# Softmax division moved behind the value products in the first attention block of a fused attention and MLP kernel

## The chip, the cores and the metric

The kernel runs on one core of a Trainium2 chip. The metric is the device time of one execution in microseconds (us); lower is better. The median of three runs of the kernel before is 956.29 us (956.23 to 956.37). Engines are named as the profile names them: PE is TensorE (matmuls), PEld its weight loads, DVE is VectorE, ACT is ScalarE, POOL is GpSimd, SP the queue that issues the DMAs.

## The reference

Three stages run one after the other: windowed causal attention with a distance penalty per head, a two-matrix MLP with a clipped gate, and a gated MLP behind an RMS norm. The change touches the attention alone.

```python
B, H, S, D = 4, 8, 576, 64            # attention; window 128
scores = q @ k.T / sqrt(D)
scores = where(0 <= i - j < 128, scores - slope[h] * |i - j|, -1e9)
attn = exp(scores - max(scores))
attn = attn / (sum(attn) + 1e-9)
x = (attn @ v) reshaped to (B*S, H*D) = (2304, 512)
h = x @ w_in                          # 512 -> 2048
x = (h * clip(h + 3, 0, 6) / 6) @ w_out
xn = x / rms(x) * rms_g
out = (silu(xn @ w_gate) * (xn @ w_val)) @ w_out2   # 512 -> 1536 -> 512
```

## The kernel before

The 2304 tokens are 18 tiles of 128 rows (`P`), in six blocks of three tiles (`BLOCKS`). For every block, attention makes the transposed input `xs` of the first MLP (four chunks `c` of 128 features, a high and a low part each), and the first MLP follows it as 16 products `ps_h` (`product1`, L484) and 16 times three products `ps_o` (`product2`, L497). Attention for the first block has nothing in front of it to run beside: it has its own loop of 15 slots (`AHEAD`, L577 to L599). Attention for the later blocks runs inside the MLP loop of the block before.

Attention goes by pairs of heads (`Pair`, index `j` from 0 to 3 in a block) and steps (`Step`, one query tile `u` of a pair against 256 keys; the first tile of a batch sees 128 keys). So the first block is 12 steps; step s belongs to pair s // 3. In slots 12 to 14 the loop also starts the three steps of the next block's first pair. A step passes through four stages, in slots that a table gives (`plan`, L437), one slot apart:

- S, slot s: `scores` (L357), two fp32 matmuls, one for each head of the pair, into `ps_s`; `bias` (L371) on DVE adds the penalty out of PSUM and takes the row extreme `m`; `exp` (L386) on ACT makes weights `t` and their row sum `den`; two instructions on POOL (L388, L389) make `r = 1 / (den + 1e-9)`.
- D, slot s + 1: `divide` (L394), two DVE instructions that multiply `t` by `r`.
- T, slot s + 2: `transpose` (L400), two or four PE transpositions of 128x128 blocks of `t` into the one bank `ps_t`; `weights` (L405) copies them to `pt` on ACT.
- V, slot s + 3: `values` (L418), two or four fp32 matmuls with 64 columns of `vraw` stationary and `pt` moving, which add into the pair's accumulator `ps_av`, already turned to features by queries. All pairs of the block use one bank, tag "A".
- With a pair's last V: `finish` (L327 on ACT, L328 on DVE) splits the accumulator into the high and low part of `xs`, and the next `vraw` but one is loaded (L297).

Each engine runs its own queue in program order, so the order of the lines in the loop is the order of the work. Within a slot of the loop before it is: scores, transpositions, values, copies of weights, bias, scaling of a coming pair's q (L304, with the loads of k and q of a later pair on SP), divisions, finish, exponentials. Behind them in slots 4, 5, 7, 8, 9 and 11 stand the pieces of `W1.step`, the conversion of the first MLP's weights: L131, L136 and L145 on ACT, L140, L143 and L147 on DVE.

An fp32 matmul stands in the trace as two records, a PE transposition as one. The two heads' matmuls of a step use different halves of the array, in `scores` the rows and in `values` the columns.

Of the kernel before, what the change touches and what calls it, by code (L numbers as in the profile page):

```python
# [10 lines left out]
F32 = mybir.dt.float32  # L11
# [4 lines left out]
AF = mybir.ActivationFunctionType  # L16
# [4 lines left out]
P = 128  # L21
# [39 lines left out]
EARLY = {0: 1, 1: 3, 2: 6, 3: 8, M2 - 1: 11}  # L61
PAIRS2 = NTILE // 6

KINDS = "QSDTLV"

OPEN = {"reuse_waits": "tile"}

# [6 lines left out]
def fused_kernel(ctx: ExitStack, tc: tile.TileContext, qd, kd, v, w1, w2, rms_g, out):  # L74
# [201 lines left out]
    class Pair:  # L276
# [17 lines left out]
        def load_v(self):  # L294
            j, k0, nk = self.j, self.lo * P, self.nch * P
            self.vr = ap.tile([P, 4, P], F32, tag="v", name="vraw", bufs=2)
            sp.dma_start(  # L297
                out=self.vr[:, : self.nch],
                in_=v[k0 : k0 + nk, j * P : (j + 1) * P].rearrange("(c p) d -> p c d", p=P),
            )  # L300

        def scale(self):
            q = self.qr[:, : self.n * P]
# [26 lines left out]
    class Step:  # L330
# [12 lines left out]
        def scores(self):  # L343
            pr, c0, k0 = self.pair, self.c0, (self.i - 1 - self.pair.lo) * P
            for x, y in PARTS_OF if pr.parts else ():
                for a, s in enumerate(self.s):
                    rows = slice(a * D, (a + 1) * D)
                    pe.matmul(  # L348
                        s[:, c0:],
                        lhsT=pr.qs[rows, x, self.u * P : (self.u + 1) * P],  # L350
                        rhs=pr.ks[rows, y, k0 + c0 : k0 + 2 * P],
                        start=(x == 0 and y == 0),
                        stop=(x == 1),
                    )
            for a, s in enumerate(self.s if not pr.parts else ()):
                rows = slice(a * D, (a + 1) * D)
                pe.matmul(  # L357
                    s[:, c0:],
                    lhsT=pr.qr[rows, self.u * P : (self.u + 1) * P],
                    rhs=pr.kr[rows, k0 + c0 : k0 + 2 * P],  # L360
                    start=True,
                    stop=True,
                )
# [16 lines left out]
                pool.memset(self.t[:, :, :HALF], 0.0)  # L380

        def exp(self):
            self.den = small.tile([P, 2], F32, tag="den", name="den")
            for a in range(2):
                p = self.t[:, a, self.p0 :]
                act.activation(p, p, AF.Exp, bias=self.m[:, a : a + 1], scale=-1.0, accum_out=self.den[:, a : a + 1])  # L386
            self.r = small.tile([P, 2], F32, tag="r", name="r")
            pool.tensor_scalar(self.r, self.den, 1e-9, None, ALU.add)  # L388
            pool.tensor_tensor(self.r, self.r, minus, ALU.pow)  # L389
# [12 lines left out]
        def weights(self):  # L402
# [3 lines left out]
            for c, sign in ((0, -1), (1, 1)) if self.joint else ():  # L406
# [2 lines left out]
                    base=c - 1, pattern=[[0, 2], [sign, P]], channel_multiplier=-sign,  # L409
                )  # L410

        def values(self):
            pr = self.pair
            if pr.acc is None:
                pr.acc = ps_a.tile([P, 3, P], F32, tag="A", name="ps_av")
            for c in range(self.from_, 2):
                for a in range(2):
                    pe.matmul(  # L418
                        pr.acc[a * D : (a + 1) * D, self.u],
                        lhsT=pr.vr[:, self.i - 1 + c - pr.lo, a * D : (a + 1) * D],  # L420
                        rhs=self.pt[:, a, c],
                        start=(c == self.from_),
                        stop=(c == 1),
                        skip_group_check=True,
                    )
# [8 lines left out]
    for k, pr in enumerate(pairs):  # L434
        b, j = divmod(k, H // 2)
        if b < 2:
            t0, plan = 3 * j if b == 0 else AHEAD - 3 + 3 * j, {"S": (0, 1, 2), "D": (1, 2, 3), "T": (2, 3, 4), "V": (3, 4, 5)}  # L437
        else:
            t0, plan = AHEAD + M1 * (b - 1) - 2 + 4 * j, {"S": (0, 0, 0), "D": (1, 1, 2), "T": (None, 2, 3), "L": (1, None, None), "V": (5, 5, 5)}
        slots["Q"].setdefault(t0 - (2 if b < 2 else 1), []).append(pr)  # L440
        for u in range(pr.n):
            step = Step(pr, u)
            for kind, at in plan.items():
                if at[u] is not None:
                    slots[kind].setdefault(t0 + at[u], []).append(step)

    def at(t):
        return [slots[kind].get(t, []) for kind in KINDS]

# [125 lines left out]
    busy(WARM)  # L575
    pairs[0].scale()
    for t in range(AHEAD):  # L577
        q, s_, d_, t_, _, v_ = at(t)
        scores(s_, t % 2)
        for x in t_:  # L580
            x.transpose()
        for x in v_:
            x.values()
        for x in t_:
            x.weights()
        for x in s_:
            x.bias()
        prepare(q, s_)
        for x in d_:
            x.divide()  # L590
        for x in v_:
            if x.last:
                finish(x.pair)
        for x in s_:
            x.exp()
        if t == 2:
            W1.load(3)
        W1.step(0, *{4: (0,), 5: (1, 2), 7: (3,), 9: (4, 5)}.get(t, ()))
        W1.step(1, *{8: (0,), 11: (1, 2)}.get(t, ()))  # L599
# [83 lines left out]
    for p, (b, m0, m1) in enumerate(PARTS):  # L683
# [13 lines left out]
        xs = xs_of[b]  # L697
        for m in range(m0, m1):
            t, slot = slot, slot + 1
            q, s_, d_, t_, l_, v_ = at(t)  # L700
            go = p < 3 or last or (t - AHEAD) % 4 in (0, 3)
            if p == 3 and m == 2:
                first.close()
# [301 lines left out]
```

## Time and profile before

| | |
|---|---|
| median of 3 runs | 956.29 us |
| span of the profiled execution | 954.2 us |
| PE busy | 937.7 us, 98% of the span |
| PE weight loads | 832.9 us, 87% |
| DVE, ACT, POOL busy | 640.5, 454.2, 186.3 us |
| the first 40th of the span: PE busy | 7 tenths; from the third 40th on 9 tenths |
| chain that ended last | PE 87%, DVE 6%, ACT 4% |

The span goes from the first instruction to the last; what the runs show above it lies around it. A busy share is the part of the span in which at least one instruction of the engine was under way. The page's view of 40 slices has each slice's busy share in tenths, about 24 us a slice. The chain of waits is followed back from the last instruction to whatever released it. A timeline row has the start, the duration of the group, engine, line, operation, and in square brackets how long the engine was idle before it and what released it.

### The profile page before, as it was taken

The numbers are of one execution on the slowest core, as the hardware profiler recorded it, in microseconds if no ns is written. First come the engines' busy times: TensorE is split into PE (matmuls) and PEld (weight loads), VectorE is DVE, ScalarE is ACT, GpSimd is POOL, SyncE is SP. The second block draws the span as 40 slices with busy tenths as digits, with TensorE's granted clock in tenths as the row PEclk, the third lists the DMA queues.
The fourth block names the chain that finished last, engine by engine and source line by source line (L and its number), as shares of the span: only waits on it lengthen the run. The fifth ranks groups of instructions, "written<-read, shape, count | busy, mean of one in ns | idle before, by whom it ended". The sixth has DMA issues, their size and how long they took to land.

```text
span 954.2 us, 14654 instructions
## 1 busy us (share of the span) xinstructions
PE 937.7 (98%) x5336; PEld 832.9 (87%) x5336; DVE 640.5 (67%) x1336; ACT 454.2 (48%) x969; POOL 186.3 (20%) x327
## 2 busy tenths in 40 slices
PE   7899999999999999999999999999999999999998
PEld 4587888888888888888899999999999999999996
DVE  5788667555878777877467657777545577545555
ACT  6899566455666655655455453433131323231120
POOL 4333012332223332422124223310000000000000
PEclk8999999999999999999999999999999999999999
DMA  6555401113666555554355757866757555755521
GB/s 231 183 194 194 187 20 51 32 53 117 198 211 203 172 164 174 164 169 130 122 182 210 287 206 293 320 229 234 249 212 281 214 202 199 265 206 211 214 86 67
DMA packets 67432, 175.02 MB, mean 183 GB/s; under 512 B 5024, under 2 KB 41888, under 8 KB 62624
## 3 DMA queue, kind: packets, MB, share of 16 engines
q1 hardware_dynamic: 67360, 174.09, 52.2%
q8 instruction: 42, 0.69, 0.3%
q14 instruction: 30, 0.25, 0.1%
HBM read 130.03 MB, written 44.04 MB: 182 GB/s over the span
## 4 chain that ended last, share of the span: by engine, by line
PE 87%; DVE 6%; ACT 4%; issue 2%; POOL 1%; ACTq 0%; POOLq 0%; DVEq 0%
PE ps_o L497 19%; PE ps_h L484 18%; PE ps_y L892 15%; PE ps_o L845 10%; PE ps_S L845 8%; PE ps_A L845 6%; PE ps_h L845 4%; PE ps_av L418 2%; PE ps_t L400 2%; PE ps_s L357 1%; DVE wx L143 1%; PE ps_s L348 1%; ACT t L386 1%; ACT wx L136 1%; DVE t L371 1%
## 5 line engine op out<-in xcount | busy, mean ns | idle before, releaser
L497 PE MATMUL ps_o<-w,g 128*128 128x512 f32 x864 | 224.0, 402 | 2.1 <-DVE w L147 1.9
L484 PE MATMUL ps_h<-xs,w 128*128 128x384 f32 x1152 | 220.2, 339 | 0.0
L484 PEld LDWEIGHTS ps_h<-xs,w 128*128 128x128 f32 x1152 | 202.4, 188 | 5.8 <-issue 0.2
L497 PEld LDWEIGHTS ps_o<-w,g 128*128 128x128 f32 x864 | 156.2, 188 | 41.1 <-issue 6.3
L892 PE MATMUL ps_y<-wo,g 128*128 128x512 f32 x648 | 150.2, 390 | 0.5 <-DVE g L881 0.5
L892 PEld LDWEIGHTS ps_y<-wo,g 128*128 128x128 f32 x648 | 121.3, 188 | 25.1 <-DVE g L881 0.9
L723 DVE SCALAR_TENSOR_TENSOR t<-t,ps_h 128x384 f32<-128x384 f32 x96 | 53.2, 554 | 98.7 <-ACT t L722 98.6
L722 ACT ACTIVATE t<-ps_h,three 128x384 f32<-128x384 f32 x96 | 55.5, 578 | 84.1 <-PE ps_h L484 80.2
L899 DVE TENSOR_TENSOR y<-y,ps_y 128x512 f32<-128x512 f32 x90 | 61.7, 686 | 35.3 <-PE ps_y L892 35.0
L386 ACT ACTIVATE t<-t,m 128x128 f32<-128x128 f32 (+1 forms) x144 | 61.4, 428 | 29.4 <-DVE t L378 14.2
L728 ACT CAST g<-t 128x384 fp32r<-128x384 f32 x96 | 49.5, 516 | 47.5 <-DVE t L723 46.2
L734 DVE TENSOR_TENSOR g<-t,g 128x384 fp32r<-128x384 f32 x96 | 54.4, 567 | 23.3 <-ACT g L728 23.0
L868 ACT ACTIVATE r<-r 128x384 f32<-128x384 f32 x36 | 19.0, 527 | 105.6 <-DVE r L867 105.6
L845 PE MATMUL ps_o<-S,tw 128*128 128x384 f32 x336 | 66.2, 339 | 0.3 <-DVE t L865 0.3
L388 POOL TENSOR_SCALAR r<-den 128x2 f32<-128x2 f32 x72 | 27.4, 380 | 187.6 <-ACT t L386 186.0
L845 PEld LDWEIGHTS ps_o<-S,tw 128*128 128x128 f32 x336 | 59.3, 188 | 1.4 <-DVE u L856 0.8
L389 POOL TENSOR_TENSOR r<-r,minus 128x2 f32<-128x2 f32 x72 | 56.0, 778 | 6.0
L407 POOL TENSOR_SCALAR_AFFINE_SELECT pt<-pt 128x256 f32<-128x256 f32 x82 | 34.5, 421 | 107.5 <-ACT pt L405 104.5
L853 ACT COPY s<-ps_S 128x384 f32<-128x384 f32 x18 | 8.7, 481 | 86.9 <-PE ps_S L845 86.9
L371 DVE CUSTOM_DVE_ANT_0 t<-ps_s,rel 128x256 f32<-128x256 f32 (+2 forms) x128 | 45.2, 395 | 3.6 <-PE ps_s L357 3.6
L143 DVE SCALAR_TENSOR_TENSOR wx<-wx,wy 128x512 uint32<-128x512 uint32 (+1 forms) x52 | 44.2, 850 | 0.0
L136 ACT ACTIVATE wx<-wraw 128x512 f32<-128x512 f32 (+1 forms) x52 | 42.8, 824 | 0.0
(138 smaller groups left out, 1471.9 us busy)
## 6 DMA issues: line engine op xcount, KB each, us to landing
tw<-t SPq DMA_DIRECT2D x52, 896.0 KB, 6.3
wraw<-w SPq DMA_DIRECT2D x36, 512.0 KB, 4.1
wo<-w SPq DMA_DIRECT2D x18, 1024.0 KB, 4.9
wraw<-w SPq DMA_DIRECT2D x16, 1024.0 KB, 9.1
t<-th SPq DMA_DIRECT2D x12, 896.0 KB, 4.3
t<-tl SPq DMA_DIRECT2D x12, 896.0 KB, 4.3
b<-wx SPq DMA_DIRECT2D x24, 256.0 KB, 2.6
w<-w SPq DMA_DIRECT2D x12, 512.0 KB, 3.0
```

What stands on the lines that cost most here:

```text
L143: vec.scalar_tensor_tensor(out=xi, in0=xi, scalar=3, in1=y, op0=ALU.logical_shift_left, op1=ALU.bitwise_or)
L371: vec.tensor_tensor_reduce(out=self.t[:, a, c0:], in0=s[:, c0:], in1=(rel_split if self.i in SPLITS else rel)[:, c0:], scale=2.0 ** (-8.0 ...
L386: act.activation(p, p, AF.Exp, bias=self.m[:, a : a + 1], scale=-1.0, accum_out=self.den[:, a : a + 1])
L389: pool.tensor_tensor(self.r, self.r, minus, ALU.pow)
L484: pe.matmul(ps[:, : n * P], lhsT=w[:, a, c * P : (c + 1) * P], rhs=xs[c][:, b, : n * P], start=(k == 0), stop=(k == 3 * KC - 1),)
L497: pe.matmul(o, lhsT=g[:, a, i * P : (i + 1) * P], rhs=w[:, b], start=(m == first and a == 0 and b == 0), stop=(m == last and a == 1),)
L722: act.activation(r[:, :nq], ps[:, :nq], AF.Relu, bias=three)
L723: vec.scalar_tensor_tensor(out=r[:, :nq], in0=r[:, :nq], scalar=6.0, in1=ps[:, :nq], op0=ALU.min, op1=ALU.mult)
L734: vec.tensor_sub(g[:, 1, :nq], r[:, :nq], f32(g[:, 0, :nq]))
L845: pe.matmul(ps, lhsT=w[a][:, k, c * P : (c + 1) * P], rhs=x[:, b, c], start=(start and j == 0), stop=(j == 5), skip_group_check=True,)
L892: pe.matmul(ps, lhsT=gs[i + k][:, a, t // 3, t % 3 * P : (t % 3 + 1) * P], rhs=wo[i + k][:, b], start=(k == 0 and a == 0 and b == 0), stop ...
L899: vec.tensor_add(acc[t], acc[t], ps)
```

## The change

In the first block alone, the weights are no longer divided before they are turned. `exp` only exponentiates, without the row sums and without the two POOL instructions. The stages are S, T, V and X in slots s, s + 1, s + 2 and s + 3. T turns the raw weights. V is `rows`: the turned weights are now stationary (128 columns), and the moving operand is 65 columns of v, 64 and a column of ones, so that each product has 128 queries as rows and the row sum in its 65th column. Three DVE instructions then add 1e-9 to the sums, take the reciprocal and scale the rows. X is `columns`: one PE transposition of the scaled 128x128 rows into the pair's accumulator, which is bank "h" for pairs 0 and 2 and bank "A" for 1 and 3. The load of v for this block writes two halves around the column of ones, in two DMAs, behind one POOL memset. The order of the lines in the loop changes with it.

```diff
         def load_v(self):
...
+            x = v[k0 : k0 + nk, j * P : (j + 1) * P].rearrange("(c p) d -> p c d", p=P)
+            if self.b:
+                sp.dma_start(out=self.vr[:, : self.nch], in_=x)
+                return
+            self.va = self.vr.rearrange("p c d -> p (c d)")[:, : self.nch * 2 * (D + 1)]
+            self.va = self.va.rearrange("p (c a d) -> p c a d", a=2, d=D + 1)
+            pool.memset(self.va[:, :, :, D:], 1.0)
+            for a in range(2):
+                sp.dma_start(out=self.va[:, :, a, :D], in_=x[:, :, a * D : (a + 1) * D])
...
         def exp(self):
+            if self.pair.b == 0:
+                for a in range(2):
+                    p = self.t[:, a, self.p0 :]
+                    act.activation(p, p, AF.Exp, bias=self.m[:, a : a + 1], scale=-1.0)
+                return
...
+        def rows(self):
+            pr = self.pair
+            ps = ps_out.tile([P, 2, D + 1], F32, tag="o2", name="ps_rows")
+            for a in range(2):
+                for c in range(self.from_, 2):
+                    pe.matmul(
+                        ps[:, a],
+                        lhsT=self.pt[:, a, c],
+                        rhs=pr.va[:, self.i - 1 + c - pr.lo, a],
+                        start=(c == self.from_),
+                        stop=(c == 1),
+                    )
+            r = small.tile([P, 2], F32, tag="r", name="r")
+            vec.tensor_scalar(r, ps[:, :, D], 1e-9, None, ALU.add)
+            vec.reciprocal(r, r)
+            self.x = gpool.tile([P, 2, D], F32, tag="g", name="rows")
+            vec.tensor_tensor(self.x, ps[:, :, :D], r.unsqueeze(2).to_broadcast([P, 2, D]), ALU.mult)
+
+        def columns(self):
+            pr = self.pair
+            if pr.acc is None:
+                p, tag = ((ps_h, "h"), (ps_a, "A"))[pr.j % 2]
+                pr.acc = p.tile([P, 4, P], F32, tag=tag, name="ps_av")[:, :3]
+            pe.transpose(pr.acc[:, self.u], self.x.rearrange("p a d -> p (a d)"), ident)
...
+            if b == 0:
+                plan = {"S": (0, 1, 2), "T": (1, 2, 3), "V": (2, 3, 4), "X": (3, 4, 5)}
...
     for t in range(AHEAD):
         scores(s_, t % 2)
+        for x in x_:
+            x.columns()
         for x in t_:
             x.transpose()
-        for x in v_:
-            x.values()
-        for x in t_:
-            x.weights()
         for x in s_:
             x.bias()
+        for x in v_:
+            x.rows()
         prepare(q, s_)
         for x in d_:
             x.divide()
-        for x in v_:
+        for x in s_:
+            x.exp()
+        for x in t_:
+            x.weights()
+        for x in x_:
             if x.last:
                 finish(x.pair)
-        for x in s_:
-            x.exp()
```

What this does to the queue of PE in slots 7 and 8, the middle of the loop, stands in the next two pieces: first before, then changed (`ps_s` scores, `ps_t` transpositions, `ps_av` values before and columns after, `ps_rows` rows; a number at a name tells buffers apart).

```order
L357 MATMUL ps_s_369<-kraw,qraw 128x256
L357 MATMUL ps_s_370<-kraw,qraw 128x256
L400 MATMUL ps_t<-ident,t 128x128 x4
L418 MATMUL ps_av<-pt,vraw 64x128 x4
L357 MATMUL ps_s_398<-kraw,qraw 128x256
L357 MATMUL ps_s_399<-kraw,qraw 128x256
L400 MATMUL ps_t<-ident,t 128x128 x2
L418 MATMUL ps_av<-pt,vraw 64x128 x4
```

The same two slots of PE's queue in the changed kernel:

```order
L362 MATMUL ps_s_380<-kraw,qraw 128x256
L362 MATMUL ps_s_381<-kraw,qraw 128x256
L446 MATMUL ps_av<-ident,rows 128x128
L410 MATMUL ps_t<-ident,t 128x128 x2
L428 MATMUL ps_rows<-vraw,pt 128x65 x4
L362 MATMUL ps_s_408<-kraw,qraw 128x256
L362 MATMUL ps_s_409<-kraw,qraw 128x256
L446 MATMUL ps_av<-ident,rows 128x128
L410 MATMUL ps_t<-ident,t 128x128 x4
L428 MATMUL ps_rows<-vraw,pt 128x65 x2
```

A transposition of the rows (L446) now stands between the scores and the transpositions of the weights. It reads what DVE made of the rows products that stand one group of scores ahead of it.

On DVE the same stretch, slot 7 and the start of slot 8, reads before (`t` and `m` are the two results of the bias, `wx` and `wy` belong to the conversion of MLP weights):

```order
L371 ISA t,m<-ps_s_369,rel 128x256
L371 ISA m 128x1
L371 ISA t,m<-ps_s_370,rel 128x256
L371 ISA m 128x1
L304 TENSOR_SCALAR qraw<-qraw,qscale 128x384
L394 TENSOR_SCALAR t<-t,r 128x128 x2
L143 SCALAR_TENSOR_TENSOR wx<-wx,wy 128x1024
L371 ISA t,m<-ps_s_398,rel 128x256
```

and in the changed kernel:

```order
L376 ISA t,m<-ps_s_380,rel 128x256
L376 ISA m 128x1
L376 ISA t,m<-ps_s_381,rel 128x256
L376 ISA m 128x1
L436 TENSOR_SCALAR r<-ps_rows 128x2
L437 RECIPROCAL r<-r 128x2
L439 TENSOR_TENSOR rows<-ps_rows,r 128x128
L309 TENSOR_SCALAR qraw<-qraw,qscale 128x384
L143 SCALAR_TENSOR_TENSOR wx<-wx,wy 128x1024
L376 ISA t,m<-ps_s_408,rel 128x256
```

The two divisions (L394) are gone; three instructions on the rows product stand behind the bias, and the conversion (L143) keeps its place ahead of the next slot's bias.

## Rows read from the trace of the kernel before

**Rows 1.** The page: the span.
```profile
span 954.2 us, 14654 instructions
```
**Rows 2.** Busy time by stretch: stretch and length, engines, granted clock, DMA share, GB/s.
```profile
5.09:38.90 33.81, 26.76 (x186) 16.20 (x185) 23.63 (x98) 25.89 (x77) 14.15 (x28) 0.85 0.53 177
38.90:105.00 66.10, 64.26 (x390) 51.72 (x389) 55.78 (x115) 59.34 (x108) 20.81 (x25) 1.00 0.64 234
105.00:900.00 795.00, 793.97 (x4511) 718.20 (x4510) 530.26 (x1069) 359.39 (x771) 148.86 (x262) 1.00 0.53 186
```
**Rows 3.** The chain that ended last, in order of time, around 30 us.
```profile
29.95 1.10 ACT t L386 x4
...
31.13 0.23 POOL r L388
...
31.43 0.72 POOL r L389
```
**Rows 4.** Waits from 5 to 39 us: us in total, times, longest.
```profile
PE ps_t L400 <- DVE t L394: 5.7, 5, 2.4
...
PE ps_t L400 <- ACT pt L405: 0.9, 1, 0.9
...
PE ps_av L418 <- DVE xs L328: 0.2, 1, 0.2
```
**Rows 5.** Busy time by stretch again, where the granted clock changes.
```profile
8.83:15.65 6.82, 6.82 (x34) 4.20 (x34) 3.95 (x20) 4.33 (x16) 2.56 (x5) 0.50 0.94 327
15.65:32.72 17.07, 11.92 (x103) 7.07 (x100) 12.89 (x50) 14.49 (x39) 7.33 (x14) 1.00 0.39 123
32.72:36.12 3.40, 3.40 (x15) 2.09 (x16) 3.05 (x12) 3.20 (x10) 1.28 (x3) 0.50 0.26 77
```
**Rows 6.** Timeline of PE from 8 to 39 us.
```profile
8.74 0.67 PE L400 MATMUL ps_t<-ident,t 128*128 128x128 f32 x2 [1.60 <-DVE t L394]
...
24.89 0.63 PE L400 MATMUL ps_t<-ident,t 128*128 128x128 f32 x4 [1.13 <-DVE t L394]
...
26.66 0.63 PE L400 MATMUL ps_t<-ident,t 128*128 128x128 f32 x4
27.21 0.66 PE L418 MATMUL ps_av<-pt,vraw 128*64 128x128 f32 x8
27.80 0.70 PE L357 MATMUL ps_s<-kraw,qraw 64*128 64x256 f32 x4
30.87 0.30 PE L400 MATMUL ps_t<-ident,t 128*128 128x128 f32 x1 [2.37 <-DVE t L394]
...
38.90 2.35 PE L484 MATMUL ps_h<-xs,w 128*128 128x384 f32 x12
```
**Rows 7.** Timeline of PE's weight loads around 20 us.
```profile
20.07 0.42 PEld L400 LDWEIGHTS ps_t<-ident,t 128*128 128x128 f32 x4 [1.28 <-ACT pt L405]
20.66 0.42 PEld L418 LDWEIGHTS ps_av<-pt,vraw 128*64 128x64 f32 x8 [0.17 <-issue]
```
**Rows 8.** Groups by line and shape on DVE, 5 to 39 us: busy us, mean ns.
```profile
L371 DVE CUSTOM_DVE_ANT_0 t<-ps_s,rel 128x256 f32<-128x256 f32 x18 | 6.9, 421 | 2.0 <-PE ps_s L357 2.0
...
L371 DVE DVE_READ_ACCUMULATOR2_ANT m<- 128x1 f32 x30 | 2.5, 84 | 0.0
...
L371 DVE CUSTOM_DVE_ANT_0 t<-ps_s,rel 128x128 f32<-128x128 f32 x8 | 2.0, 285 | 1.6 <-PE ps_s L357 1.6
...
L147 DVE TENSOR_TENSOR w<-wx,w 128x1024 fp32r<-128x1024 f32 x1 | 1.2, 1226 | 1.5 <-ACT w L145 1.5
L143 DVE SCALAR_TENSOR_TENSOR wx<-wx,wy 128x1024 uint32<-128x1024 uint32 x1 | 1.2, 1219 | 0.0
```
**Rows 9.** Timeline of DVE at 143 us: an instruction that reads its neighbour's result.
```profile
143.10 0.42 DVE L371 CUSTOM_DVE_ANT_0 t<-ps_s,rel 128x256 f32<-128x256 f32 x1
...
143.57 0.42 DVE L378 TENSOR_TENSOR t<-t 128x256 f32<-128x256 f32 x1
```
**Rows 10.** DMA issues from 0 to 60 us: count, KB each, median us to landing.
```profile
vraw<-v SPq DMA_DIRECT2D x4, 192.0 KB, 3.5
```

More of the change, by code (lines that the diff above doesn't have):

```diff
@@ L62 @@
 PAIRS2 = NTILE // 6
-KINDS = "QSDTLV"
+KINDS = "QSDTLVX"
 OPEN = {"reuse_waits": "tile"}
@@ L296, in load_v @@
             self.vr = ap.tile([P, 4, P], F32, tag="v", name="vraw", bufs=2)
[L297 to L300, printed above, removed]
+            x = v[k0 : k0 + nk, j * P : (j + 1) * P].rearrange("(c p) d -> p c d", p=P)
[7 more added lines that the diff above has]
+                sp.dma_start(out=self.va[:, :, a, :D], in_=x[:, :, a * D : (a + 1) * D])
         def scale(self):
@@ L577, in fused_kernel @@
     for t in range(AHEAD):
-        q, s_, d_, t_, _, v_ = at(t)
+        q, s_, d_, t_, _, v_, x_ = at(t)
         scores(s_, t % 2)
+        for x in x_:
+            x.columns()
         for x in t_:
             x.transpose()
-        for x in v_:
-            x.values()
-        for x in t_:
-            x.weights()
         for x in s_:
             x.bias()
+        for x in v_:
+            x.rows()
         prepare(q, s_)
@@ L699, in fused_kernel @@
             t, slot = slot, slot + 1
-            q, s_, d_, t_, l_, v_ = at(t)
+            q, s_, d_, t_, l_, v_, _ = at(t)
             go = p < 3 or last or (t - AHEAD) % 4 in (0, 3)
```

## Prediction, made before the changed kernel ran

> **What bounds the kernel now.** I read the busy times by stretch first. From 105 us to 900 us PE is busy for 793.97 of 795 us [rows 2], so time lost or won ahead of that stretch is not made up later. The first block's attention is the stretch from the first scores at 5.09 us to the first MLP product at 38.90 us [rows 2, 6]: 33.81 us, in which PE shows 26.76 us of work at a mean granted clock of 0.85. It is the only place that the change touches. From 38.90 to 105 us PE is busy for 64.26 of 66.10 us, and the work there hangs on the slots behind the loop, so it shifts as a whole when the loop ends earlier or later.
>
> Next the chain of waits inside the loop. It alternates: exponential on ACT, then the two POOL instructions (0.23 and 0.72 us), then a division on DVE, then PE [rows 3]. The waits say the same: PE's transpositions waited 5.7 us for divisions and 0.9 us for copies, its value products 0.2 us for the split of the accumulator [rows 4], 6.8 us in all. The rest of the loss is the clock: for 6.82 and 3.40 us the granted clock was 0.50, that is 1.2 instead of 2.4 GHz, with PE busy throughout [rows 5]. Each time the fall came after PE had sat idle for long, 1.60 and 2.37 us; an idle of 1.13 us was not followed by one [rows 6].
>
> **The change part by part.** All prices are for the full clock; a step has eight records of value products if it sees two key chunks, four if it sees one (8 and 4 of the 12 steps).
>
> *Removed wait.* The division leaves the way from exponential to transposition: at most the 6.8 us [rows 4]. The second accumulator bank is in this number with its 0.2 us and can be worth no more.
>
> *Rows in place of values.* Eight value records with 64 stationary columns load in 0.42 us; four transpositions, with 128 stationary columns, need the same 0.42 us [rows 7]. So a record with 128 stationary columns takes 0.105 us where one with 64 takes 0.053. The new products have 128 stationary columns and stream 65. If the load sets the pace, eight records take 0.84 us instead of 0.42: 8 x 0.42 + 4 x 0.21 = +4.2 us. Lower bound: the transpositions' pace comes from streaming 128 columns, the loads are hidden, and 65 columns cost no more than now: 0. Upper bound: load and stream one after the other, 0.16 us a record: +8.5 us. I take 4.2, because the row with the same stationary shape is the transposition's. The Trainium skill, page "TensorE: Matmul & The Clock Gate", section "LDWEIGHTS (loading the stationary operand)", speaks against the change here: the time of a load goes with the columns of the stationary operand, about columns / 1.2 in ns, so 107 ns for 128 columns and 53 for 64. By that rule the term is 4.3 us and the time 960.3; by the streaming reading it is 0 and the time 956.0.
>
> *Turning the rows.* One transposition for each step, 0.105 us, and the 0.17 us that a group with its own wait spends on issue [rows 7]: 12 x 0.28 = +3.3 us. Without the issue time it would be 1.3.
>
> *The new wait.* The turn (L446) stands at the head of the slot, in front of the transpositions and the rows, and needs DVE's three instructions on the rows product issued just before. A group of PE delivers 0.24 us after its last load (0.66 against 0.42) [rows 6, 7]. On DVE, reading PSUM takes 421 ns at 256 columns and 285 at 128 [rows 8]; carried down to 2 columns that is an estimated 0.15 us each for the addition and the reciprocal, and 0.285 for the scaling. A reader of its neighbour's result starts 0.05 us after that ends [rows 9]. So 0.24 + 0.15 + 0.05 + 0.15 + 0.05 + 0.285, and about 0.07 for each of two hand-overs: 1.07 us. Between lies only the next group of scores, 0.43 us of issue (0.70 less the drain [rows 6]), 0.21 if narrow, with 0.17 us before and after it. PE idles 0.30 us in nine slots and 0.52 in three: +4.3 us. Bounds: 1.6 us less if the two small ones cost 84 ns, as the smallest DVE row does [rows 8]; 3.6 more if the reciprocal takes three times 0.15. The transpositions and rows queue behind this turn, and the next scores behind those.
>
> *Conversion on DVE.* L143 and L147 (1.22 and 1.23 us [rows 8]) stay between one slot's scaling and the next slot's bias. Before, they ran while PE waited anyway. Now each holds up the bias and with it the next rows' scaling, for which PE waits: about 0.95 us each after what the scores hide, +1.9. Bounds 0 and 2.4.
>
> *Left-over waits of the transpositions.* The first follows the second scores at once and waits for its exponential, the second for the copy of the first (one bank `ps_t`), the last for a division of the next block: +1.5, between 1 and 2.
>
> *End of the loop.* The last split now stands on ACT behind two exponentials and a copy, and the first MLP product needs it for its last quarter: +0.6, between 0 and 1.
>
> *The clock.* The two long idles disappear, since the first transposition no longer stands behind two divisions; no idle in the sums above passes 1.2 us. I take PE to keep 2.4 GHz, which halves 10.2 us: -5.1. This is an upper bound of the gain, as part of the slow work lay under other waits; the lower bound is 0.
>
> *Counted as nothing.* The row sums on ACT, 24 POOL instructions and 24 divisions go: the cover is that ACT and POOL are then off the way, and DVE has the new three in their place. The four POOL memsets run on an emptied POOL, and the four extra DMA issues on SP stand behind loads of k and q. A load of v lands 3.5 us after issue [rows 10] and is needed three slots later, over 6 us; if that cover went, each late load would hold PE by the difference.
>
> **Sum.** -6.8 + 4.2 + 3.3 + 4.3 + 1.9 + 1.5 + 0.6 - 5.1 = +3.9 us on the profiled span of 954.2 [rows 1], so 958.1. The median of the runs lies 2.1 us above that span, with no part of it touched: 960.2 us.
>
> **The rivals.**
>
> *Weight loads hidden.* PE loads the next weights beside the running product, and the 65 columns cost what the values did. For it: later in the trace loads are busy for 718 of 795 us beside a PE that is busy throughout [rows 2]. Against: the transpositions' pace. The sum falls by 4.2 to 956.0, no change. It decides at a spacing of 0.053 against 0.105 us. Chance 0.15.
>
> *The division is back in time* (the other sign). If the way from the last rows record to the scaled rows takes 0.77 us or less, not 1.07, the scores and their issue cover it; PE then never stands in front of the turn and the 4.3 goes, and with that slack the conversion's 1.9 as well: 954.0, faster by 0.24%. For it: DVE rows of 84 ns exist. Against: with two of these the way is still 0.94 us. Chance 0.09.
>
> *The clock falls again.* PE works with short pauses in every slot and may be granted 1.2 GHz as before. One stretch like the shorter one costs 1.7 us (961.9), all 10.2 us cost 5.1 (965.3). [...] Against: from 15.65 to 32.72 us, with a transposition group in every slot, the granted clock was 1.00 [rows 5]. Chance 0.18.
>
> *The change does not shorten the way:* v in two halves lands late. Four loads, each 0.5 us late, would add 2 us: 962.2. Chance 0.03.
>
> **How the numbers follow.** 0.2% is 1.9 us, about what a measurement of this kernel can tell from no change. The forecast, 960.2, has 0.55, and its own bounds reach from 957 to 964; a twentieth of that chance lies below 958.2. Faster: 0.09. Same: the hidden loads and that twentieth, 0.18. Slower: the rest, 0.73. The range takes in the hidden loads below and one slow stretch with dear loads above: 955.8 to 964.5. It leaves out the faster rival and the clock slow throughout.
>
> **What would show it.** Right: PE waits of `ps_av` L446 on `rows` L439 of some 0.3 us in nearly every slot, summing to 4 to 7 us; loads of L428 spaced by 0.105 us, eight in about 0.85; no POOL in the chain; a granted clock of 1.00 in the loop; the first `ps_h` product near 42.2 us. Wrong: L428 spaced by 0.053 us, or L446 without idle time before it; or a product that starts before 38 us. If the clock falls, the stretches show it.

## The result and the profile after

| | before | after |
|---|---|---|
| median of 11 runs each, us | 956.35 (955.19 to 957.65) | 960.95 |
| ratio, 95% interval | 1 | 1.0057 (1.0039 to 1.0075) |
| span of the profiled execution, us | 954.2 [rows 1] | 958.2, of a run of 959.92 |

The changed kernel is slower by 0.57%, about 5 us. Of its eleven runs one took 1314 us and is left out of the ratio, as are single runs of 3224 us in run 4 and 983 us in run 5 below; seven lie between 959.1 and 961.7 us and three between 965.4 and 966.8 us, a spread that the kernel before doesn't show.

First the page of the changed kernel: its span, and the chain that ended last by engine.

```profile
span 958.2 us, 14624 instructions
...
PE 87%; DVE 7%; ACT 4%; issue 1%; POOL 0%; ACTq 0%; POOLq 0%; DVEq 0%
```

POOL, which [rows 3] show in the chain of the loop, has 0% of it, after 1% before. Next its busy time by stretch, cut at the first scores, the first MLP product and the two changes of the granted clock (columns as in [rows 2]).

```profile
5.13:40.82 35.69, 29.09 (x198) 21.59 (x197) 23.97 (x111) 23.34 (x53) 2.25 (x7) 0.95 0.50 165
40.82:105.00 64.18, 62.50 (x368) 50.65 (x367) 53.63 (x113) 56.17 (x104) 20.34 (x23) 0.97 0.63 233
105.00:900.00 795.00, 793.67 (x4509) 716.59 (x4508) 530.49 (x1068) 360.11 (x772) 146.80 (x262) 1.00 0.53 185
...
5.13:37.50 32.37, 25.80 (x184) 19.14 (x183) 21.94 (x100) 22.62 (x51) 0.99 (x4) 1.00 0.55 181
37.50:44.30 6.80, 6.78 (x27) 5.93 (x26) 3.11 (x13) 2.35 (x9) 2.18 (x6) 0.50 0.50 154
```

From 105 to 900 us nothing changed. The loop is 35.69 us long instead of 33.81 [rows 2], and where the kernel before had two stretches at half the clock inside it [rows 5], this one has a single stretch of 6.80 us, which begins in the loop and ends in the first MLP product. The timeline of PE (start, length, instruction, count, idle time before it) shows a plain slot, the long idles with the transpositions of slots 9 (25.35 us) and 11 (31.65 us) behind them, and that product:

```profile
10.33 0.33 PE L446 MATMUL ps_av<-ident,rows 128*128 128x128 f32 x1 [0.36 <-DVE rows L439]
10.49 0.60 PE L410 MATMUL ps_t<-ident,t 128*128 128x128 f32 x4
10.93 1.00 PE L428 MATMUL ps_rows<-vraw,pt 128*128 128x65 f32 x8
11.86 0.70 PE L362 MATMUL ps_s<-kraw,qraw 64*128 64x256 f32 x4
12.71 0.33 PE L446 MATMUL ps_av<-ident,rows 128*128 128x128 f32 x1
...
24.83 0.33 PE L446 MATMUL ps_av<-ident,rows 128*128 128x128 f32 x1 [1.16 <-DVE rows L439]
25.35 0.66 PE L410 MATMUL ps_t<-ident,t 128*128 128x128 f32 x4 [0.20 <-ACT pt L415]
...
31.34 0.33 PE L446 MATMUL ps_av<-ident,rows 128*128 128x128 f32 x1 [1.58 <-DVE rows L439]
31.65 0.66 PE L410 MATMUL ps_t<-ident,t 128*128 128x128 f32 x4
...
36.37 0.33 PE L446 MATMUL ps_av<-ident,rows 128*128 128x128 f32 x1 [0.65 <-DVE rows L439]
37.08 1.61 PE L428 MATMUL ps_rows<-vraw,pt 128*128 128x65 f32 x8 [0.38 <-ACT pt L415]
...
40.82 3.94 PE L522 MATMUL ps_h<-xs,w 128*128 128x384 f32 x12
44.60 0.60 PE L410 MATMUL ps_t<-ident,t 128*128 128x128 f32 x4
```

Eight rows products take 0.93 us from start to start (10.93 to 11.86), the eight value products took 0.59 [rows 6]. The first MLP product starts 1.92 us later than before [rows 6] but takes 3.94 us instead of 2.35. The transposition behind it is 3.51 us later than in the kernel before, whose row is this:

```profile
41.09 0.60 PE L400 MATMUL ps_t<-ident,t 128*128 128x128 f32 x4
```

The waits from 5 to 46 us (us in total, times, longest), and behind the 1.58 us of idle the chain around 28 us:

```profile
PE ps_av L446 <- DVE rows L439: 4.6, 6, 1.6
...
PE ps_t L410 <- ACT pt L415: 0.6, 2, 0.4
...
PE ps_rows L428 <- ACT pt L415: 0.4, 1, 0.4
...
PE ps_t L410 <- ACT t L391: 0.2, 1, 0.2
```

```profile
27.79 0.96 ACT w L145
28.77 1.23 DVE w L147
30.00 0.33 DVE t L376
```

DVE stood first for ACT's half of the weight conversion (L145) and then took 1.23 us for its own (L147); the bias and the scaling of the rows came behind both.

### The profile page after: what moved, and what is told of

Its sections match the earlier page's. It is cut to its first block, busy times and chain, and to the rows that moved or that the text cites. A ratio compares the mean times of both kernels' runs of the same rounds, so it can differ in the third digit from the quotient of the medians.

```text
span 958.2 us, 14624 instructions
## 1 busy us (share of the span) xinstructions
PE 942.1 (98%) x5348; PEld 839.7 (88%) x5348; DVE 641.7 (67%) x1348; ACT 451.0 (47%) x945; POOL 172.1 (18%) x307
## 4 chain that ended last, share of the span: by engine, by line
PE 87%; DVE 7%; ACT 4%; issue 1%; POOL 0%; ACTq 0%; POOLq 0%; DVEq 0%
PE ps_o L535 18%; PE ps_h L522 18%; PE ps_y L932 15%; PE ps_o L885 10%; PE ps_S L885 8%; PE ps_A L885 6%; PE ps_h L885 4%; PE ps_av L454 2%; PE ps_t L410 2%; PE ps_s L362 1%; DVE wx L143 1%; ACT wx L136 1%; PE ps_s L353 1%; DVE t L763 1%; PE ps_x L588 1%
## 5 line engine op out<-in xcount | busy, mean ns | idle before, releaser
L396 ACT ACTIVATE t<-t,m 128x128 f32<-128x128 f32 (+2 forms) x120 | 50.0, 418 | 27.6 <-DVE t L383 14.5
L398 POOL TENSOR_SCALAR r<-den 128x2 f32<-128x2 f32 x60 | 23.6, 393 | 186.7 <-ACT t L396 185.1
L399 POOL TENSOR_TENSOR r<-r,minus 128x2 f32<-128x2 f32 x60 | 47.2, 786 | 5.0
L143 DVE SCALAR_TENSOR_TENSOR wx<-wx,wy 128x512 uint32<-128x512 uint32 (+1 forms) x52 | 44.2, 850 | 0.0
```

The costliest lines, as they stand in the source:

```text
L143: vec.scalar_tensor_tensor(out=xi, in0=xi, scalar=3, in1=y, op0=ALU.logical_shift_left, op1=ALU.bitwise_or)
```

## Experiments

Theory 1 at the outset: the turn at the head of the slot makes PE wait for DVE, and the rows products pay for their 128 stationary columns. Theory 2: the clock decides. The rival throughout: one round through PE, DVE and ACT sets the slot, and a wait that is taken away comes back elsewhere. Ratios are against the kernel before, with 95% intervals.

| run | median us | ratio |
|---|---|---|
| 1 turn behind the transpositions | 961.8 | 1.0078 (1.0052 to 1.0103) |
| 2 turn of a constant | 961.3 | 1.0049 (1.0037 to 1.0061) |
| 3 filler matmuls | 964.8 | 1.0096 (1.0083 to 1.0109) |
| 4 kernel before, two accumulator banks | 955.8 | 0.9997 (0.9988 to 1.0006) |
| 5 rows products twice | 963.5 | 1.0079 (1.0061 to 1.0096) |
| 6 rows products in halves | 958.4 | 1.0025 (1.0016 to 1.0034) |
| 7 copy in front of the exponentials | 960.5 | 1.0060 (1.0032 to 1.0088) |
| 8 runs 1 and 7 together | 961.6 | 1.0060 (1.0035 to 1.0084) |
| 9 conversion spread | 958.8 | 1.0037 (1.0015 to 1.0059) |
| 10 runs 1, 6 and 7 together | 957.0 | 1.0009 (1.0001 to 1.0018) |
| 11 runs 1, 6, 7 and 9 together | 954.8 | 0.9988 (0.9980 to 0.9997) |
| 12 kernel before, conversion spread | 956.0 | 0.9995 (0.9986 to 1.0004) |

**Run 1.**

```
-        for x in x_: x.columns()
         for x in t_: x.transpose()
+        for x in x_: x.columns()
```

> The turn (columns) stands behind the slot's transpositions instead of in front of them; same instructions, same output. Theory 1 (the wait of the turn for DVE, at the head of the slot, is paid in time): the transpositions, 0.43 us and their 0.17 us of issue, cover the short idles of 0.36 to 0.65 us in front of L446; the two behind the conversions (1.16 and 1.58 us) shrink by 0.5 each. The PE idle in front of L446 falls from 4.6 to about 1.5 us and the time by 2 to 3 us, to 958 to 959 us. Rival (another wait takes its place): the transpositions now come at the head and wait for the exponential of the slot before, L391, or for the copy L415 of the one bank ps_t; the sum of PE's waits in the loop stays near 5.7 us and the time within 1 us of 960.9.

PE's idle in front of L446 went, all of it, and in its place stood this wait from 5 to 46 us:

```profile
PE ps_t L410 <- ACT pt L415: 5.8, 6, 1.9
```

The transpositions now headed the slot and waited for the copy that empties their one bank. Up to slot 9 the run was 0.4 us ahead of the changed kernel (the transposition at 24.96 against 25.35 us); then the granted clock was 0.50 for at least 12.8 us, from 31.40 to 44.20. The rival was right: PE's waits in the loop came to 6.5 us, and the time stayed within 1 us. How much of that is the new wait and how much the longer slow stretch, this run doesn't separate.

**Run 2.**

```
-            pe.transpose(pr.acc[:, self.u], self.x.rearrange("p a d -> p (a d)"), ident)
+            pe.transpose(pr.acc[:, self.u], rel[:, :P], ident)
```

> The turn takes 128 columns of the constant rel instead of the scaled rows: the same instruction at the same place, without its wait for DVE. The attention output of the first block is left out of what follows. Theory 1: all of the 4.6 us of PE idle in front of L446 goes; part comes back in the rows products, which wait for DVE to empty their one bank; 3 to 4.5 us less, 956.5 to 958 us. Rival (the added PE work is all of the loss, waits only move): at most 1 us less, 960 us, with the idle in front of the rows products or of the transpositions.

No PE wait for DVE is left in front of the turn, and the time is the same. Its waits, the transposition of slot 9 and its stretch at the low clock:

```profile
PE ps_t L410 <- ACT pt L415: 2.8, 3, 1.6
```

```profile
24.57 0.66 PE L410 MATMUL ps_t<-ident,t 128*128 128x128 f32 x4 [1.64 <-ACT pt L415]
```

```profile
26.10:45.60 19.50, 19.45 (x79) 15.64 (x79) 11.07 (x45) 10.28 (x27) 3.16 (x7) 0.50 0.29 89
```

At the transposition of slot 9 it leads the changed kernel by only 0.78 us (24.57 against 25.35), although the changed kernel's PE had by then idled 2.37 us in front of the turn (0.36 + 0.36 + 0.49 + 1.16): behind the wait for the turn stood the next one, for the copy, 1.64 us long. Theory 1 falls as it stood: up to there 2.4 us of idle behind one releaser were worth 0.8 us. What the other 2.2 us were worth is not shown, since PE soon ran 19.5 us and more at half the clock.

**Run 3.**

```
+        if t in FILLER:  # {11: 12, 13: 4}
+            p, tag = (ps_a, "A") if t == 11 else (ps_h, "h")
+            warm = p.tile([P, 4 * P], F32, tag=tag, name="warm")
+            busy(FILLER[t])
```

> Twelve matmuls on a constant into a free accumulator bank in slot 11 and four in slot 13, in front of the turn, where PE idled 1.58 and 0.65 us: 0.107 us each at full clock, so 1.28 and 0.43 us, inside the idles. Theory 2 (the fall of the clock at the end of the loop follows from these idles and costs half of 6.8 us): the granted clock stays at 1.00 from 5 to 105 us and the time falls by 2.5 to 3.4 us, to 957.5 to 958.5 us. Rival (the clock falls by something else, or the slow stretch lies under other waits): a stretch at 0.50 is still there or the first ps_h product starts no earlier; 960.5 to 961.5 us.

A miss, and a test badly sized: a filler is two records, together 0.46 us at full clock and not 0.107 (the eight records in slot 13 take 1.83 us from start to start), and the clock had fallen at about 26.5 us, before the first of them.

```profile
31.22 6.45 PE L612 MATMUL warm<-rel 128*128 128x256 f32 x24
```

The clock was 0.50 for the first 2 us of these records, until about 33.2 us, and 1.00 for the rest; the turn behind them came at 37.50 us, where the changed kernel has it at 31.34. The run shows that the fall is not bound to one place: the same program up to slot 10 had no fall before 37.5 us in the profile of the changed kernel. Whether a filler of the right size would hold the clock was not tried.

**Run 4.**

```
-                pr.acc = ps_a.tile([P, 3, P], F32, tag="A", name="ps_av")
+                p, tag = (ps_h, "h") if pr.b == 0 and pr.j % 2 == 0 else (ps_a, "A")
+                pr.acc = p.tile([P, 4, P], F32, tag=tag, name="ps_av")[:, :3]
```

> The kernel before, with the accumulator of the first block's pairs in the banks h and A in turn and nothing else changed: the second part of the change alone. Theory (the bank is worth no more than the 0.2 us that PE waited for its split): 0 to 0.3 us less than before, 956.0 to 956.4 us. Rival (the wait was short in the record but moved the long waits, or the clock, behind it): over 1 us off either way.

As expected: the second bank alone can't be told from no change.

**Run 5.**

```
-            for a in range(2):
+            for a in (0, 1, 0, 1):
                 for c in range(self.from_, 2):
                     pe.matmul(ps[:, a], lhsT=self.pt[:, a, c], ...)
```

> Every rows product is issued twice (the second time over the first, so the result is the same): 80 more records with 128 stationary and 65 moving columns. Theory 1 (the load sets the pace, 0.105 us a record): 80 x 0.105 = 8.4 us more PE work; PE's waits hide at most the wait of the copy, since the turn waits for the rows: first ps_h product 6.5 to 8.5 us later than in the changed kernel at the same clock. Rival (loads hidden, 0.053 us): 4.2 us. Second rival (the slot is set by ACT and DVE, PE has room): under 3 us.

Timeline, with the transposition of slot 11, and stretch of the loop:

```profile
11.08 1.90 PE L428 MATMUL ps_rows<-vraw,pt 128*128 128x65 f32 x16
12.91 0.70 PE L362 MATMUL ps_s<-kraw,qraw 64*128 64x256 f32 x4
...
35.20 0.60 PE L410 MATMUL ps_t<-ident,t 128*128 128x128 f32 x4
```

```profile
5.13:44.60 39.47, 35.59 (x277) 29.27 (x277) 23.98 (x109) 23.15 (x52) 2.25 (x7) 1.00 0.47 151
```

Sixteen records take 1.83 us from start to start, so the 0.90 us of eight more is 0.113 us each: the price that theory 1 gave a record. Yet 80 of them, 9.0 us, made the profiled span only 2.6 us longer (960.8 against 958.2). Two things took up the rest. The first is the waits: up to the transposition of slot 11, at full clock in both profiles, 60 added records, 6.8 us, made the loop 3.55 us longer (35.20 against 31.65). The second is the clock, which was 1.00 throughout: the first product starts 3.78 us later and then runs at full speed. So the time is the second rival's, and its reason holds in part: PE had room for about half of the added work.

**Run 6.**

```
-                    pe.matmul(ps[:, a], lhsT=self.pt[:, a, c], ...)
+                    for q in (0, D):
+                        pe.matmul(ps[q : q + D, a], lhsT=self.pt[:, a, c, q : q + D], ...)
```

> Each rows product in two, with 64 of the 128 queries as stationary columns: twice the records, the same columns loaded in all, twice the columns streamed. Theory 1 (a record costs its load): a record takes 0.053 us, eight become sixteen in about 0.85 us, the time within 1 us of the changed kernel. Rival (a record of 65 moving columns has a fixed price of about 0.11 us, whatever is loaded): sixteen in 1.75 us, 8 to 9 us more work and a time of 966 or more.

Timeline of PE's loads, then of PE:

```profile
11.02 0.55 PEld L429 LDWEIGHTS ps_rows<-vraw,pt 128*64 128x64 f32 x16 [0.17 <-issue]
```

```profile
11.02 0.69 PE L429 MATMUL ps_rows<-vraw,pt 128*64 128x65 f32 x16
11.64 0.70 PE L362 MATMUL ps_s<-kraw,qraw 64*128 64x256 f32 x4
```

Both expectations missed. Sixteen records with 64 stationary columns took 0.62 us from start to start, less than the eight with 128 (0.93), and nearly the 0.59 of the value products before. The median fell by 2.6 us against the changed kernel's. In the profile the lead is 0.65 us at the transposition of slot 11 (31.00 against 31.65) and 1.5 us on the span, while PE's waits in front of the turn rose from 4.6 to 5.3 us. So a record is not priced by its columns alone: two halves that write different output partitions cost less than the whole. Whether the smaller operand or the change of output partitions from record to record does it, no run separates. The Trainium skill, page "TensorE: Matmul & The Clock Gate", section "Part 3: Packing small matmuls — row/col tiling", has matmuls on different parts of the array overlap, which the 0.62 us fit. By the Trainium skill, the same page, "TensorE: Matmul & The Clock Gate", section "LDWEIGHTS (loading the stationary operand)", a load of 64 columns takes about 53 ns, so sixteen one after the other would take an estimated 0.85 us; the measured 0.62 decides against reading it as a spacing.

**Run 7.**

```
+        for x in t_: x.weights()
         for x in s_: x.exp()
-        for x in t_: x.weights()
```

> On ACT the copy of the transposed weights (L415) stands in front of the slot's exponentials instead of behind them. Theory 3 (PE's waits in this loop are those of one round through PE, DVE and ACT; what one order takes away another gives back): the exponentials end 0.35 to 0.56 us later in the slots where they were ready first; the transpositions wait for L391 instead, the 0.6 us of waits for L415 goes; the time within 1 us of 960.9. Rival (the order of ACT was the change's mistake): 2 us or more faster.

Within 1 us of the changed kernel by the medians, and the waits for L415 went as theory 3 had it. But the single runs go from 956.8 to 970.6 us, and five of the eleven lie below the changed kernel's lowest, 959.08: that ACT's order alone is worth nothing is not shown.

**Run 8.** Run 1's edit and run 7's together.

> Both: the turn behind the transpositions, and the copy in front of the exponentials. With the turn later PE waited 5.8 us for copies L415 that stood behind exponentials and conversions on ACT. Theory 3: that wait goes for the slots without a conversion, in front of the transpositions stands a wait for L391 of 0.2 to 0.4 us; PE's waits in the loop 3 to 4 us; at the clock of the changed kernel 1.5 to 2.5 us less, 958.5 to 959.5; with falls of the clock up to 962. Rival (the conversions on ACT alone set the wait): waits for L415 or L391 of 1.5 us or more in two or three slots stay as they are, no gain.

Half a hit. The waits for the copy are gone and the profiled span is 955.2 us, 3.0 below the changed kernel's, with waits of 1.04 and 1.23 us for the exponential L391 left at the two conversions. The median is not lower; single spans run from 955.2 to 964.9 us. Why the same program differs by 10 us is not settled by this run.

**Run 9.**

```
-        vec.scalar_tensor_tensor(out=xi, in0=xi, ...)        # L143
-        t = yield x
+        for s in (slice(0, n // 2), slice(n // 2, n)) if spread else (slice(0, n),):
+            vec.scalar_tensor_tensor(out=xi[:, s], in0=xi[:, s], ...)
+            t = yield x
...
-        vec.tensor_sub(t[:, 1], x, f32(t[:, 0]))              # L147
+        (pool if spread else vec).tensor_sub(t[:, 1], x, f32(t[:, 0]))
```

`spread` holds for the first weight unit; its stage 3 stands in slots 6 and 7.

> The changed kernel, with the two long DVE instructions of the first weight conversion taken out of DVE's way: L143 in two halves, in slots 6 and 7, and L147 on POOL, which is idle there. Theory (the conversions cost the 1.9 us of the prediction): PE's idles of 1.16 and 1.58 us in front of L446 fall to 0.5 us or less each, the loop ends 1.5 to 2 us earlier at the same clock; and if no fall of the clock follows, 3 us more: 956 to 959 us. Rival (ACT's share of the conversion, L136 and L145 in front of the exponentials, holds the slot just as long): the idles stay over 1 us with another releaser, less than 0.5 us gained.

The idles in slots 9 and 11 fell from 1.16 and 1.58 us to 0.63 and to none, and the wait in front of the turn from 4.6 to 2.4 us in all. At the transposition of slot 11 the run led by 2.3 us (29.33 against 31.65), but at the first product by 0.6 (40.22), not 1.5 to 2, for two reasons. The clock fell here too, and 4 us earlier: it was 0.50 from 33.50 to beyond 41.10 us, with no idle of PE over 0.63 us in the loop before. And the subtraction on POOL held DVE; the timelines of DVE and of POOL:

```profile
29.02 1.63 DVE L312 TENSOR_SCALAR qraw<-qraw,qscale 128x384 f32<-128x384 f32 x1
```

```profile
28.08 2.35 POOL L150 TENSOR_TENSOR w<-wx,w 128x1024 fp32r<-128x1024 f32 x1 [6.76 <-ACT w L148]
```

The scaling of q, 0.41 us elsewhere, ended at 30.65 us, POOL's subtraction at 30.43. The median, 958.8 us, lies in the range expected, but that range was given for a clock that does not fall.

**Run 10.** The edits of runs 1, 6 and 7.

> The rows products in two halves of 64 queries (3.0 us less PE work by the profile of that run: 0.61 against 0.93 us of issue in eight slots, 0.38 against 0.49 in four), the turn behind the transpositions, the copy in front of the exponentials. Theory: with the turn out of the head of the slot the shorter products shorten the slot: first transposition of the next block 2 to 3 us earlier than without the halves (41.90 us), 953 to 956 us. Rival (the slot is set by ACT and DVE, exponential and copy, by now): the waits of the transpositions for L391 grow by what the products lose, under 1 us gained.

957.0 us, 1 above the range expected and 4.0 below the changed kernel; the first transposition of the next block is at 43.37 us in the profiled run, where 39 to 40 was expected. Half the clock cost the profiled run some 3.5 us, in a way that is told in the last section. Against run 8 the median fell by 4.7 us, but the fastest runs of the two differ by 1.2 (955.69 and 956.87). From the transposition of slot 6 to that of slot 11 both profiles are at full clock; run 8 first, then run 10:

```profile
16.37 0.83 PE L410 MATMUL ps_t<-ident,t 128*128 128x128 f32 x4 [0.22 <-ACT t L391]
...
29.83 0.84 PE L410 MATMUL ps_t<-ident,t 128*128 128x128 f32 x4 [1.23 <-ACT t L391]
```

```profile
18.42 0.83 PE L410 MATMUL ps_t<-ident,t 128*128 128x128 f32 x4 [0.34 <-ACT t L391]
...
31.68 0.84 PE L410 MATMUL ps_t<-ident,t 128*128 128x128 f32 x4 [1.45 <-ACT t L391]
```

That is 13.46 us in run 8 and 13.26 here, while the waits for L391 grow from 2.9 to 3.8 us: in this stretch the rival was right, and the halves gain 0.2 us. How much of the 4.7 us is theirs and how much belongs to the spread of run 8 is not settled.

**Run 11.** The edits of runs 1, 6, 7 and 9.

> All four edits: halves, turn later, copy first, conversion spread. Theory: the parts add: 2 to 3 us below the run without the spread conversion, 951.5 to 954.5 us, faster than the kernel before by 0.2 to 0.5%. Rival (the clock falls in any order of this loop and takes back what the order gains): a stretch at 0.50 of 3 us or more, and a time within 0.2% of the kernel before.

954.8 us: faster than both kernels, by 0.12% (0.03 to 0.20) than the one before. That is less than the 0.2% that the prediction took for about what a measurement can tell, 0.3 us above the range expected, and in time what the rival gave, though without its stretch at 0.50. The loop and its waits:

```profile
5.13:36.34 31.21, 25.97 (x277) 16.41 (x277) 23.84 (x109) 23.36 (x52) 4.61 (x8) 1.00 0.59 191
```

```profile
PE ps_t L413 <- ACT t L394: 2.7, 8, 0.5
...
PE ps_av L451 <- DVE rows L444: 1.1, 1, 1.1
```

No wait longer than 1.1 us is left, the clock is 1.00 to the end of the loop, and the first product starts 2.56 us earlier than before [rows 6]. From the transposition of slot 6 to that of slot 11 the run needs 11.26 us (16.02 to 27.28), 2.0 less than run 10: this is what the spread conversion gives there. Of the eleven spans nine lie between 952.7 and 953.5 us. That the kept clock makes them close is not shown: run 7 has single runs at a mean clock of 1.00 at 956.8 and at 970.6 us.

**Run 12.**

> The kernel before, with the conversion spread as in the two runs before (L143's work in two halves in slots 6 and 7, L147's on POOL) and nothing else. Theory (the long idles of the loop belong to the conversion, in either kernel): the idles of 1.13 and 2.37 us in front of the transpositions fall by 0.6 and 1.2 us, one fall of the clock less, 953 to 954.8 us; then the lead of the run with all four edits is the conversion's and not the new softmax's. Rival (the division holds the transpositions in any case, and POOL, now busy for 4 us with the subtraction, holds back the reciprocals behind it): no gain, 955.5 to 958 us.

The edit is run 9's, in the kernel before. No gain: the rival was right, and more directly than it said. POOL's subtraction stood from 28.15 to 30.5 us, and the division on DVE, which is what PE waits for, stood beside it:

```profile
28.22 2.54 DVE L397 TENSOR_SCALAR t<-t,r 128x128 f32<-128x128 f32 x2 [0.61 <-POOL r L392]
```

The first of the two idles did fall, from 1.13 to 0.60 us; the second stayed, at 2.43. Both falls of the clock stayed as well, the first of them by the lengths of the groups alone (last section). So run 11's lead is not the spread conversion's alone: the kernel before can't use it this way.

## Why the prediction was right, and which of its steps were not

Forecast 960.2 us, measured 960.95, inside the range, on the side that had 0.73. The sum was near by luck: it had errors of opposite sign, work and waits 1.7 and 1.95 us too dear, the clock's gain 3.4 us too high. Luck has a part in the last step too, the 2.1 us from span to median: the time of each run of the two kernels lies 1.7 us above its own span, and the measured median lies 1.0 above the profiled run. The profiled loops give three parts: PE's work at full clock (its busy time less half of the stretches at 0.50), PE's idle time, and what the low clock cost.

| part, us | predicted | measured |
|---|---|---|
| work: rows products, turns | 4.2 + 3.3 = +7.5 | 27.43 - 21.65 = +5.8 |
| waits: old ones gone, turn, conversion, left-over, end | -6.8 + 4.3 + 1.9 + 1.5 + 0.6 = +1.5 | 6.60 - 7.05 = -0.45 |
| clock | -5.1 | 3.4 - 5.1 = -1.7 |
| sum | +3.9 | +3.6 |

Work before is 26.76 - 10.22 / 2, after it is 29.09 - 3.32 / 2; idle is length less busy time [rows 2]; the clock after is half of 6.80 us, of which half lies in the first product. Against this sum stand 3.5 us at the next transposition and 4.0 on the span.

- **The step that failed is the clock**: "I take PE to keep 2.4 GHz". It fell once, at 37.50 us, after idles of 0.65 and 0.38 us and some 6 us after the long one of 1.58; the rule that I drew from two cases, that a fall follows an idle over 1.2 us, was too narrow: in run 9 the clock fell with no idle over 0.63 us in the loop. By its own terms the prediction had no ground for it either, since 0.30 us of the new wait and 0.95 of the conversion already make an idle of 1.25. Of the 5.1 us that the clock cost before, 3.4 were lost again: the rival that the clock falls again came true in part.
- **Rows products**: the spacing was right (0.113 us a record in run 5 against 0.105); that the stationary columns set it holds for whole products alone, as run 6 shows. The term was too dear: 0.34 us more in a slot of eight and 0.13 in one of four, 3.2 us and not 4.2, perhaps because the 0.17 us of issue in front of the value products [rows 7] is hidden now, which no run isolates.
- **Turn**: 0.16 to 0.17 us from its start to the next group's, 2.0 for twelve and not 3.3. In five slots 0.15 us of idle stands in front of it without a wait in the list (scores that end at 12.56, the turn at 12.71); the table has it among the waits. With the rows products this makes 5.2 of the 5.8 us of work; the rest is not accounted for.
- **New wait**: 4.6 us against 4.3 and the conversion's 1.9. DVE's three instructions were estimated well (0.15, 0.15 and 0.285 against 159, 166 and 292 ns below). But it is not 0.3 us in nearly every slot: three idles of 0.36 to 0.49, one of 0.65 and the two behind the conversions make it up.

```profile
L439 DVE TENSOR_TENSOR rows<-ps_rows,r 128x128 f32<-128x128 f32 x12 | 3.5, 292 | 0.4
...
L437 DVE RECIPROCAL r<-r 128x2 f32<-128x2 f32 x12 | 2.0, 166 | 0.4
...
L436 DVE TENSOR_SCALAR r<-ps_rows 128x2 f32<-128x2 f32 x12 | 1.9, 159 | 6.3 <-PE ps_rows L428 6.3
```

- **That the wait is the price** is what runs 1 and 2 speak against: without it the time stayed, though with a longer slow stretch. At full clock, up to slot 9, 2.4 us of it were worth 0.8, since the next wait stood right behind; for the other 2.2 us no run shows it.
- **Left-over waits** came to 1.2 us (0.6 + 0.4 + 0.2) for the predicted 1.5; the end of the loop cost nothing, probably since the slow first product hid it (in run 5, at full clock, that product waited 0.17 us for the split on ACT).
- **Other rivals**: hidden loads are excluded by run 5; the division back in time by the idles in front of L446; no wait for v is in the list. The signs named for a right forecast held for the sum in front of L446, for eight rows products (0.93 us for 0.85) and for POOL's absence; they failed for the clock and for the first product (42.2 foreseen, 40.82 measured).

What stays open: three of the changed kernel's ten runs took about 5 us more, at a mean granted clock of 0.998 to 0.999, where the profiled one has 0.996. No profile of such a run was had.

## What to carry to other kernels

Where several engines hand one piece of work round, price a wait by the distance to the next wait and not by its length; the cheap test is to feed the waiting instruction with a constant, and to compare up to the first change of the clock. The edits here that moved idle time about moved the fall of the clock too, to places between 26 and 37.5 us, so a span mixes the two. Work that PE does in its waits is cheaper than it looks: here 6.8 us of it cost 3.55 at the same clock. Before a reduction is moved to another form, look at what the stationary operand then is: halving it into two output ranges brought eight products from 0.93 to 0.62 us, after 0.59 before, and the median 2.6 us down.

## What the hardware showed unexpectedly

**A granted clock that reads 1.00 while PE works at half speed.** In run 10's profile, timeline of PE and stretch:

```profile
7.57 1.23 PE L362 MATMUL ps_s<-kraw,qraw 64*128 64x256 f32 x4
8.73 1.11 PE L410 MATMUL ps_t<-ident,t 128*128 128x128 f32 x4
...
15.88 0.70 PE L362 MATMUL ps_s<-kraw,qraw 64*128 64x256 f32 x4
```

```profile
7.57:14.62 7.05, 7.05 (x47) 4.62 (x46) 2.88 (x17) 3.74 (x9) 0.00 (x0) 1.00 0.86 299
```

The same four scores took 1.23 us and later 0.70, the ratio seen elsewhere between 0.50 and 1.00 ([rows 5]: from 8.83 to 15.65 us), and PE had no idle time in the stretch. Run 12's profile shows the same:

```profile
11.87 1.23 PE L360 MATMUL ps_s<-kraw,qraw 64*128 64x256 f32 x4
```

```profile
8.80:15.50 6.70, 6.65 (x34) 4.12 (x34) 4.10 (x20) 4.05 (x14) 2.62 (x6) 1.00 0.92 333
```

So the lengths of equal groups tell the clock more surely than its row, and the 957.0 us of run 10's span, 3.0 above the lowest of the same kernel, have a likely cause: 7.05 us at half speed are 3.5 us. That the dear runs of the changed kernel, with their high mean clock, are of this kind is a guess that no profile here shows.

**POOL stops some instructions of DVE.** Run 9's scaling took 1.63 us instead of 0.41, run 11's 1.82, and run 12's two divisions 2.54 us instead of 0.56, each ending 0.2 to 0.3 us behind POOL's subtraction; in run 11 PE's scores of slot 12 waited 0.64 us for that scaling. The three instructions on the rows ran beside the same subtraction in their usual 0.16, 0.17 and 0.29 us, in run 9 as in run 11. The Trainium skill, page "SBUF — State Buffer", section "Who interferes with whom", says that the two share a port pair which one instruction holds to its end, and names `tensor_scalar`, the operation of the scaling and the divisions, among those that can take it; the traces agree.
